# Cached attention for one token: head loops on every engine, wo's first rows in seven loads, the result stored as four rows

## The chip, the cores and the metric

The kernel runs on one core of one Trainium2 chip. The metric is the device time of one execution in microseconds (us); the median of several runs is compared. The profile comes from one more execution, taken by the hardware profiler. The engines are PE (TensorE), DVE (VectorE), ACT (ScalarE), POOL (GpSimd) and SP (SyncE, which here only issues DMAs). ACT issues a few DMAs too. The core has 16 DMA engines.

## What is computed

One decode step for one token x of 576 numbers. Its layernorm xn goes through two branches, and both are added to x. All data are float32.

```python
q = (xn @ wq).reshape(32 heads, 128)                       # wq: 576 x 4096
scores = einsum("hd,hkd->hk", q, k_cache) * 128 ** -0.5     # k_cache: 32 x 16384 x 128
o = einsum("hk,hkd->hd", softmax(scores), v_cache)          # v_cache: 32 x 16384 x 128
attention = o.reshape(4096) @ wo                            # wo: 4096 x 576
geglu = (gelu(xn @ w_gate) * (xn @ w_up)) @ w_down          # 576 x 4608, 576 x 4608, 4608 x 576
out = x + attention + geglu
```

K and V are 8.39 MB for each head, 537 MB for 32 heads; the weights make up the rest of the 587.6 MB that the kernel reads. Each number is used once.

## The kernel before, in words

Three SBUF slots of 64 KB per partition (`slot_a`, `slot_b`, `slot_v`, lines 124 to 126) take everything that is loaded. A load fills 128 partitions; partition p of a head holds its positions 128p to 128p + 127, 64 KB in one piece.

**Order.** There is no scheduler: the class `Order` (line 39) works out for each instruction which semaphores it must wait for, and hangs the last wait on the instruction itself; earlier ones become instructions of their own (line 91 and line 106). SP issues its DMAs in program order, so a DMA that waits holds up all that stand behind it.

**Projections (lines 224 to 327).** The weights wq, w_gate and w_up come into the slots; PE multiplies them with xn spread over 32 columns. q stays in PSUM (`qb`). `ffn` writes gate and up, and `ffn_act` (line 319) makes `hT` = gelu(gate) * up on DVE and ACT.

**Heads (lines 342 to 394).** K of the even heads comes into `slot_b`, of the odd ones into `slot_a`, V into `slot_v`. SP's order is K(0) as two halves of 64 columns, K(1), V(0), K(2), V(1) and so on: K(h+2) waits until DVE has read K(h), V(h) until PE has read V(h-1). For each head:

- DVE multiplies the slot by q, broadcast from `qs` (two halves, one for even and one for odd heads), and sums over 128 columns into `scores` (line 368 and 369, recorded at line 214); then `reduce_max` (line 384) and, after a transpose on PE, the maximum of one row (line 386).
- ACT copies the sums of the head before from PSUM (`z`), copies the next q to `qs`, scales the maximum (`nb`), takes exp into `pe` with its sum in `lsum`, copies the output column of the head before to `oall` and fetches the q after next (`qcur`).
- PE runs a hardware loop of 32 turns already (line 342): q broadcast (line 334, `pqs`), transpose (line 346), the maximum broadcast, the diagonal sums of the head before (`out_steps`, line 329), and 32 products of `pe` with V (`po`, line 334).

DVE, ACT and SP have all 32 heads written out one after the other. `hold` (line 137) puts the start of DVE's code on a multiple of 128 instructions and arms a hint for the branch in `release` (line 143), a loop of two turns at the end; line 160 aligns SP's code in the same way.

**Tail (lines 396 to 468).** w_down's first 28 rows per partition go to `slot_b`, where DVE sums them weighted with `hT`; V(31) follows, then the last 8 rows of w_down and wo, in pieces of 8, 12, 4, 4, 2, 1 and 1 rows per partition (`WO_PIECES`, line 32). One row is 576 numbers, 2304 bytes. PE multiplies each row with its column of `hT` or `oT` (`add_out`, line 435). DVE copies the sums (four rows of 144 numbers, on partitions 0, 32, 64 and 96) to `o4`, and SP and ACT store two rows each, with one DMA. SP then waits for both (line 134).

Of the kernel before, what the change touches and what calls it, by code (L numbers as in the profile page):

```python
# [10 lines left out]
ALU = mybir.AluOpType  # L11
# [19 lines left out]
WD_A = 28  # L31
WO_PIECES = (8, 12, 4, 4, 2, 1, 1)
WO_A = 20
# [84 lines left out]
@with_exitstack  # L118
def kernel(ctx: ExitStack, tc: tile.TileContext, x, k_cache, v_cache, wq, wo, wg, wu, wd, out):
    nc = tc.nc  # L120
    ends = tc.alloc_semaphore("ends")
    slots = []
    for i, name in enumerate(("slot_a", "slot_b", "slot_v")):
        t = nc.alloc_sbuf_tensor_at(name, [P, R * DH], F32, offset=SLOT_AT + i * SLOT_B)
        SIZES[t.name] = R * DH
        slots.append(t.ap())
    i = nc.sync.dma_start(slots[0], wq[:DM].rearrange("(p j) f -> p (j f)", j=DJ)).then_inc(ends, 32)
# [6 lines left out]
    nc.sync.wait_ge(ends, 32)  # L134


def hold(engine):

    engine.addr_align(128, offset=0, max_nops=0)
    return engine.mark_branch_hint_location()  # L140


def release(nc, kind, engine, place):
    only = OrderedEngineSet([kind])
    name = f"release_{nc.next_id()}"
    turns = nc.alloc_registers(f"{name}_i", engines=only)
    nc.regs_mov(turns, 0)
    nc.br(f"{name}_loop", engines=only)
    with nc.body(f"{name}_loop", valid_engines=only):
        engine.nop()  # L150
        nc.regs_alu(turns, turns, 1, op=ALU.add)
        engine.br_lt(turns, 2, on_true=f"{name}_loop", on_false=f"{name}_end").branch_hint(place)
    nc.switch_bb(f"{name}_end")


def decode(tc, x, k_cache, v_cache, wq, wo, wg, wu, wd, out, slots, s_ends):
    nc = tc.nc
    o = Order(tc)
    place = hold(nc.vector)
    nc.sync.addr_align(128, offset=0, max_nops=0)  # L160
    names = iter(range(1000))
# [31 lines left out]
    z = sbuf("z", P, 512)  # L193
    qcur, qs = sbuf("qcur", 1, DH), sbuf("qs", P, 2 * DH)
    S = sbuf("scores", P, 2 * R)
    lsum, oall = sbuf("lsum", P, H), sbuf("oall", P, H)
    gu, hT = sbuf("gu", P, 2 * WD_T), sbuf("hT", P, WD_T)
# [27 lines left out]
    ROW3 = 3 * DF  # L225
    nc.tensor.wait_ge(s_ends, 32).then_inc(s_ends, -32)
    qt = load(sb[:, ROW3 : ROW3 + QS], wtail["q"])
# [15 lines left out]
    o.op("vector", lambda e: e.memset(eps_t, EPS), eps_t)  # L243
    for bank in (PO, pc, pq):
        o.op("vector", lambda e, bank=bank: e.memset(bank, 0.0), bank)
    dve("tensor_reduce", par, ident.rearrange("p (d s) -> p s d", s=2), axis=AX.X, op=ALU.add)
# [45 lines left out]

    def q_of(h):
        return qs[:, h % 2 * DH : h % 2 * DH + DH]

    s_q, s_m, s_n, s_o, s_e, s_v = (tc.alloc_semaphore(f"to_pe_{n}") for n in "qmnoev")
    act(qcur, q_part(0))
    pe_op(pq[:, :DH], ones[:1, :], qcur, True, True)
    act(q_of(0), pq[:, :DH])
    act(qcur, q_part(1), signal=s_q)  # L300

# [30 lines left out]
    def chain(steps):  # L332
        for k, (dst, lhs, rhs, start, stop) in enumerate(steps):
            i = nc.tensor.matmul(dst, lhs, rhs, start=start, stop=stop)  # L334
        return i.then_inc(o.sem["tensor"], 1)

    def take(s, n=1):
        nc.tensor.wait_ge(s, n).then_inc(s, -n)  # L338

    o.wait("tensor", [ident, ones, same], [pg, pc, PO, pq])  # L340
    base, marks = o.count["tensor"], 5
    with nc.Fori(0, H, engines=OrderedEngineSet([mybir.EngineType.PE]), head_slot={mybir.EngineType.PE: 0}):
        take(s_q)
        chain([(pq[:, :DH], ones[:1, :], qcur, True, True)])
        take(s_m)
        nc.tensor.transpose(pt[:1, :P], pm, ident).then_inc(o.sem["tensor"], 1)  # L346
        take(s_n)
        chain([(pb[:, :1], ones[:1, :], nm[:1], True, True)])
        take(s_o)
        chain(out_steps(0))  # L350
        take(s_e)
        take(s_v, 16)
        chain([(PO[32 * (k % 4) : 32 * (k % 4) + 4, :], pe[:, 4 * k : 4 * k + 4], sv[:, 512 * k : 512 * k + 512], k < 4, k >= 28)
               for k in range(32)])
    o.count["tensor"] = base + marks * H

    def ran(h, mark, out, *ins):
        o.note("tensor", o.sem["tensor"], base + marks * h + mark, ins, [out])

    s_k = [sem() for _ in range(2)]  # L360
    times = [0, 0]
    for h in range(H):
        s = h % 2
        kt, n = (sb, sa)[s], R if h else SUB
        for i in range(0, R, n):
            if h:
                times[s] += 16
            part = kt[:, i * DH : (i + n) * DH]
            o.dma(part, kv[h][:, i * DH : (i + n) * DH], s_k[s] if h else sem(), times[s] or 16)
        if h:  # L370
            o.dma(sv, vv[h - 1], s_v, 0)
            ran(h - 1, 5, PO, pe, sv)
        sc = S[:, s * R : s * R + R]
        for i in range(0, R, n):
            blk = kt[:, i * DH : (i + n) * DH].rearrange("p (n d) -> p n d", d=DH)
            dve("tensor_mul", blk, blk, q_of(h).unsqueeze(1).to_broadcast([P, n, DH]))
            dve("tensor_reduce", sc[:, i : i + n], blk, axis=AX.X, op=ALU.add)
        if h == 0:
            ffn_act()
        act(z, PO, signal=s_o)  # L380
        ran(h, 1, pq[:, :DH], ones, qcur)
        if h + 1 < H:
            act(q_of(h + 1), pq[:, :DH])
        o.op("vector", lambda e: e.reduce_max(pm, sc, axis=AX.X), pm, sc, signal=s_m)
        ran(h, 2, pt[:1, :P], pm, ident)
        o.op("vector", lambda e: e.tensor_reduce(nm[:1], pt[:1, :P], axis=AX.X, op=ALU.max, negate=True), nm[:1], pt[:1, :P], signal=s_n)  # L386
        ran(h, 3, pb[:, :1], nm[:1])
        act(nb, pb[:, :1], scale=SCALE)
        act(pe, sc, AF.Exp, signal=s_e, bias=nb, scale=SCALE, accum_out=lsum[:, h : h + 1])
        ran(h, 4, pc[:, :1], z, same)  # L390
        if h:
            act(oall[:, h - 1 : h], pc[:, :1])
        if h + 1 < H:
            act(qcur, q_part(min(h + 2, H - 1)), signal=s_q)
# [10 lines left out]
    o.dma(sv, vv[H - 1], s_v, 0)  # L405
    ran(H - 1, 5, PO, pe, sv)
    wd_rows = load_rows(sa, 0, wdv, WD_A, WD_T - WD_A)
    wo_rows, lo = [], 0
    for n in WO_PIECES:
        wo_rows += load_rows(sa, WD_T - WD_A + lo, wov, lo, n) if lo < WO_A else load_rows(sb, 1 + lo - WO_A, wov, lo, n)  # L410
        lo += n

    act(z, PO)
    for s in out_steps(H - 1):
        pe_op(*s)
    act(oall[:, H - 1 :], pc[:, :1])

# [3 lines left out]
    dve("reciprocal", rl, pl)  # L421
    dve("tensor_mul", on, oall, rl)
    dve("tensor_mul", onx.rearrange("p (h r) -> p h r", r=4), on.unsqueeze(2).to_broadcast([P, H, 4]),
# [68 lines left out]
```

## Time and profile before

| what | us |
|---|---|
| median of 3 runs (1364.1 to 1364.12) | 1364.12 |
| the profiled execution | 1364.24 |
| its span, first to last instruction | 1362.5 |
| outside the span | 1.74 |
| DVE busy | 1158.3 |
| PE busy | 444.2 |
| ACT busy | 63.2 |

The read rate over the span is 431 GB/s. In the rows of the profile, `L214` is line 214 of the kernel; since helpers record the operations, many rows share a line, and the names of the tiles (out<-in) tell them apart. PEld is the loading of weights into PE, SPq and ACTq are the DMA queues of SP and ACT, PEq is PE's sequencer. Idle time of an engine stands with what ended it. The DMA share is the mean busy share of the 16 DMA engines; in short stretches it can be over 1, since a packet is counted where it starts or ends.

### The profile page before, as it was taken

What the parts mean: (1) busy time and instruction counts of PE and PEld (TensorE: products, weight loads), DVE (VectorE), ACT (ScalarE), POOL (GpSimd) and SP (SyncE); (2) the same over time, 40 slices, a digit from 0 to 9 for tenths busy, and PEclk for the clock granted to TensorE, in tenths of its full rate; (3) what the DMA queues carried; (4) which work ended last, traced back from release to release, by engine and by line L of the source; (5) the groups of instructions that cost most, each with busy time, mean ns of one, the idle gap of its engine ahead of it and who ended that gap; (6) DMA issues with size and microseconds to landing.
All of it is one profiled execution on the core that took longest, in us unless ns stands there. A gap on an engine that the chain in (4) does not pass through costs nothing.

```text
span 1362.5 us, 6978 instructions
## 1 busy us (share of the span) xinstructions
PE 444.2 (33%) x3012; PEld 161.2 (12%) x3012; DVE 1158.3 (85%) x195; ACT 63.2 (5%) x231; POOL 1.0 (0%) x7
## 2 busy tenths in 40 slices
PE   2431233332322333323222333333223333232236
PEld 1110111110101111101111111001111111011112
DVE  1069999899888888899888888998888888988882
ACT  0000000000000000000000000000000000000000
POOL 0000000000000000000000000000000000000000
PEclk9675666666556666665556666665566666665569
DMA  9999999999999999999999999999999999999998
GB/s 402 445 426 435 444 435 433 433 431 433 433 433 433 439 439 435 435 431 433 433 431 433 433 444 435 433 433 433 433 433 433 433 439 439 435 433 431 434 432 347
DMA packets 11831, 587.72 MB, mean 431 GB/s; under 512 B 1319, under 2 KB 1325, under 8 KB 1710
## 3 DMA queue, kind: packets, MB, share of 16 engines
q1 hardware_dynamic: 11812, 587.60, 99.6%
q8 instruction: 5, 0.08, 0.0%
q14 instruction: 4, 0.03, 0.0%
q10 hardware_dynamic: 10, 0.01, 0.0%
HBM read 587.60 MB, written 0.00 MB: 431 GB/s over the span
## 4 chain that ended last, share of the span: by engine, by line
DMA 49%; DVE 39%; issue 0%; PE 0%; DVEq 0%
DMA slot_b<-in_A_k_cache_dram 43%; DVE slot_b L214 20%; DVE scores L214 19%; DMA slot_b<-in_B_w_down_dram 3%; DMA slot_b<-in_A_wo_dram 3%; PE pg L211 0%; PE pg L346 0%; DVE z L214 0%; DVEq L91 0%; DVE nm L386 0%
## 5 line engine op out<-in xcount | busy, mean ns | idle before, releaser
L334 PE MATMUL po<-slot_v,pe 128*4 128x512 f32 x2048 | 292.9, 736 | 607.4 <-PEq L338 607.4
L214 DVE TENSOR_TENSOR slot_a<-slot_a,qs 128x16384 f32<-128x16384 f32 x16 | 275.6, 17223 | 42.6 <-DMA slot_a<-in_A_k_cache_dram 42.6
L214 DVE TENSOR_TENSOR slot_b<-slot_b,qs 128x16384 f32<-128x16384 f32 (+1 forms) x17 | 275.7, 16218 | 39.2 <-DMA slot_b<-in_A_k_cache_dram 39.2
L214 DVE TENSOR_REDUCE scores<-slot_b 128x128 f32<-128x16384 f32 (+1 forms) x17 | 275.7, 16216 | 0.6
L214 DVE TENSOR_REDUCE scores<-slot_a 128x128 f32<-128x16384 f32 x16 | 275.5, 17220 | 0.6
L334 PEld LDWEIGHTS po<-slot_v,pe 128*4 128x4 f32 x2048 | 56.5, 99 | 816.8 <-issue 816.8
L346 PE MATMUL pg<-ident,pm 128*1 128x128 f32 x32 | 11.9, 371 | 240.0 <-PEq L338 240.0
L219 ACT ACTIVATE z<-po 128x512 f32<-128x512 f32 x33 | 19.7, 597 | 889.1 <-PE po L334 889.1
L334 PE MATMUL pc<-same,z 128*128 128x1 f32 x256 | 59.8, 355 | 0.0
L334 PEld LDWEIGHTS pc<-same,z 128*128 128x128 f32 x256 | 57.1, 328 | 0.5
L214 DVE TENSOR_TENSOR slot_v<-pg,same 128x396 f32<-128x396 f32 (+1 forms) x6 | 3.4, 558 | 51.7 <-PE pg L211 51.5
L346 PEld LDWEIGHTS pg<-ident,pm 128*1 128x1 f32 x32 | 2.5, 79 | 245.2 <-issue 245.2
L386 DVE TENSOR_REDUCE nm<-pg 1x1 f32<-1x128 f32 x32 | 8.9, 279 | 17.8 <-PE pg L346 17.8
L214 DVE SCALAR_TENSOR_TENSOR slot_b<-slot_b,hT 128x576 f32<-128x576 f32 x27 | 22.1, 819 | 0.9
L334 PE MATMUL pg<-nm,ones 1*128 1x1 f32 x64 | 17.6, 342 | 14.8 <-PEq L338 14.8
L334 PEld LDWEIGHTS pg<-nm,ones 1*128 1x128 f32 x64 | 15.8, 306 | 24.2 <-issue 24.2
L219 ACT ACTIVATE nb<-pg 128x1 f32<-128x1 f32 x32 | 5.5, 171 | 237.1 <-PE pg L334 237.1
L334 PE MATMUL pqs<-qcur,ones 1*128 1x128 f32 x64 | 15.4, 321 | 1.3 <-PEq L338 1.3
L211 PE MATMUL pg<-slot_b,z 128*32 128x396 f32 (+1 forms) x72 | 8.8, 660 | 17.5 <-DMA slot_b<-in_B_w_gate_dram 17.5
L219 ACT ACTIVATE pe<-scores,nb 128x128 f32<-128x128 f32 x32 | 12.9, 402 | 1.0
L334 PEld LDWEIGHTS pqs<-qcur,ones 1*128 1x128 f32 x64 | 9.4, 182 | 28.7 <-issue 28.7
L214 DVE COPY small<-pc 128x5 f32<-128x5 f32 x1 | 0.2, 164 | 13.1 <-PE pc L211 13.1
(75 smaller groups left out, 119.9 us busy)
## 6 DMA issues: line engine op xcount, KB each, us to landing
slot_b<-in_A_k_cache_dram SPq DMA_DIRECT2D x2, 4096.0 KB, 22.8
slot_b<-in_B_w_down_dram SPq DMA_DIRECT2D x1, 8064.0 KB, 42.4
slot_b<-in_B_w_gate_dram SPq DMA_DIRECT2D x1, 6912.0 KB, 54.9
slot_a<-in_B_w_up_dram SPq DMA_DIRECT2D x1, 6912.0 KB, 38.1
slot_a<-in_A_wo_dram SPq DMA_DIRECT2D x1, 3456.0 KB, 41.3
slot_v<-in_B_w_gate_dram SPq DMA_DIRECT2D x1, 2304.0 KB, 28.6
slot_v<-in_B_w_up_dram SPq DMA_DIRECT2D x1, 2304.0 KB, 36.9
slot_a<-in_B_w_down_dram SPq DMA_DIRECT2D x1, 2304.0 KB, 28.5
```

Of the source, the lines that this page charges most:

```text
L211: o.op("tensor", lambda e: e.matmul(outp, lhsT, rhs, start=start, stop=stop), outp, lhsT, rhs, signal=signal)
L214: o.op("vector", lambda e: getattr(e, name)(out, *ins, **kw), out, *[a for a in ins if isinstance(a, bass.AP)], *[a for a in kw.values() i ...
L219: o.op("scalar", lambda e: e.activation(out, src, func, **kw), out, src, kw.get("bias") if isinstance(kw.get("bias"), bass.AP) else None, ...
L334: i = nc.tensor.matmul(dst, lhs, rhs, start=start, stop=stop)
L346: nc.tensor.transpose(pt[:1, :P], pm, ident).then_inc(o.sem["tensor"], 1)
L386: o.op("vector", lambda e: e.tensor_reduce(nm[:1], pt[:1, :P], axis=AX.X, op=ALU.max, negate=True), nm[:1], pt[:1, :P], signal=s_n)
```

## The change

The change writes the heads as hardware loops on SP (two heads a turn, 15 turns), DVE (two heads a turn, 16 turns) and ACT (five loops, cut where q's row in PSUM changes), beside the one that PE has. Inside a loop the waits are explicit: `take` waits for a semaphore and takes its count down again, as an instruction of its own. Addresses that depend on the turn come from registers. With that:

- K(0) is one load, and `ffn_act` stands ahead of the heads.
- `qs` has one half; ACT writes it after DVE's multiplication of the head before (`s_qf`).
- PE ends each head with a drain that tells SP that V is read (`s_vf`); `po` itself tells ACT (`s_po`).
- `oall` has a column more, since the first turn writes an empty one.
- The aligned starts of DVE and SP are gone; DVE and ACT have the hint and the `release` loop, which now stands after the stores.
- wo's first 8 rows per partition are two pieces of 4. The first of these comes by seven loads: partitions 0 to 29 in five loads of six, partitions 30 and 31 in one, partitions 32 to 127 in one.
- Each of the four rows of the result is stored by a DMA of its own, two from SP and two from ACT; the semaphore at the end counts to 64.

The core of the diff:

```diff
-WO_PIECES = (8, 12, 4, 4, 2, 1, 1)
+WO_PIECES = (4, 4, 12, 4, 4, 2, 1, 1)
+WO_LOW = (0, 6, 12, 18, 24, 30, 32, P)
...
-    place = hold(nc.vector)
-    nc.sync.addr_align(128, offset=0, max_nops=0)
+    places = [e.mark_branch_hint_location() for e in (nc.vector, nc.scalar)]
...
-    kv = k_cache.rearrange("b h (p n) d -> (b h) p (n d)", p=P)
-    vv = v_cache.rearrange("b h (p n) d -> (b h) p (n d)", p=P)
+    kv, vv = (c.rearrange("b h (p n) d -> p (b h) (n d)", p=P) for c in (k_cache, v_cache))
...
+    def take(e, s, n=1):
+        e.wait_ge(s, n).then_inc(s, -n)
...
+    ffn_act()
...
+    def load_k(h, dst, s):
+        nc.sync.dma_start(dst, kv[:, head(h), :].rearrange("p h f -> p (h f)")).then_inc(s_k[s], 16)
+
+    def load_v(h):
+        nc.sync.dma_start(sv, vv[:, head(h), :].rearrange("p h f -> p (h f)")).then_inc(s_v, 16)
+
+    for h, dst in ((0, sb), (1, sa)):
+        o.wait("sync", [], [dst])
+        load_k(h, dst, h)
+    o.wait("sync", [], [sv])
+    load_v(0)
+    with nc.sync.Fori(0, (H - 2) // 2) as i:
+        for s, dst in ((0, sb), (1, sa)):
+            take(nc.sync, s_kf)
+            load_k(i * 2 + (2 + s), dst, s)
+            take(nc.sync, s_vf)
+            load_v(i * 2 + (1 + s))
+
+    with nc.Fori(0, H, engines=OrderedEngineSet([KIND["tensor"]]), head_slot={KIND["tensor"]: 0}):
...
         chain([(PO[32 * (k % 4) : 32 * (k % 4) + 4, :], pe[:, 4 * k : 4 * k + 4], sv[:, 512 * k : 512 * k + 512], k < 4, k >= 28)
-               for k in range(32)])
+               for k in range(32)], s_po)
+        nc.tensor.drain().then_inc(s_vf, 1)
+
+    with nc.vector.Fori(0, H // 2):
+        for s, kt in ((0, sb), (1, sa)):
+            blk = kt.rearrange("p (n d) -> p n d", d=DH)
+            sc = S[:, s * R : s * R + R]
+            take(nc.vector, s_k[s], 16)
+            take(nc.vector, s_qd)
+            nc.vector.tensor_mul(blk, blk, qs.unsqueeze(1).to_broadcast([P, R, DH])).then_inc(s_d, 1)
+            nc.vector.wait_ge(s_d, 1).then_inc(s_qf, 1)
+            nc.vector.tensor_reduce(sc, blk, axis=AX.X, op=ALU.add).then_inc(s_d, 1)
+            nc.vector.wait_ge(s_d, 2).then_inc(s_kf, 1)
+            take(nc.vector, s_d, 2)
+            nc.vector.reduce_max(pm, sc, axis=AX.X).then_inc(s_m, 1)
+            take(nc.vector, s_pt)
+            nc.vector.tensor_reduce(nm[:1], pt[:1, :P], axis=AX.X, op=ALU.max, negate=True).then_inc(s_n, 1)
+
+    for h0, n in ((0, 6), (6, 8), (14, 8), (22, 8), (30, 2)):
+        row, lo = divmod(min(h0 + 2, H - 1), H // 4)
+        with nc.scalar.Fori(0, n) as i:
+            take(nc.scalar, s_po)
+            nc.scalar.activation(z, PO, AF.Copy).then_inc(s_o, 1)
+            take(nc.scalar, s_pq)
+            take(nc.scalar, s_qf)
+            nc.scalar.activation(qs, pq[:, :DH], AF.Copy).then_inc(s_qd, 1)
+            take(nc.scalar, s_pb)
+            nc.scalar.activation(nb, pb[:, :1], AF.Copy, scale=SCALE).then_inc(s_a, 1)
+            take(nc.scalar, s_a)
+            nc.scalar.activation(pe, S[:, bass.ds(i % 2 * R, R)], AF.Exp, bias=nb, scale=SCALE, accum_out=lsum[:, bass.ds(i + h0, 1)]).then_inc(s_e, 1)
+            take(nc.scalar, s_pc)
+            nc.scalar.activation(oall[:, bass.ds(i + h0, 1)], pc[:, :1], AF.Copy)
...
-    def load_rows(t, at, src, lo, n):
-        load(t[:, at * D : (at + n) * D], src[:, lo * D : (lo + n) * D])
+    def load_rows(t, at, src, lo, n, cuts=(0, P)):
+        for a, b in zip(cuts, cuts[1:]):
+            load(t[a:b, at * D : (at + n) * D], src[a:b, lo * D : (lo + n) * D])
...
+    take(nc.sync, s_kf)
     first = load_rows(sb, 0, wdv, 0, WD_A)
...
-    release(nc, mybir.EngineType.DVE, nc.vector, place)
-    for g in range(2):
-        o.dma(of[:, 2 * g * QUART : 2 * (g + 1) * QUART].rearrange("o (a f) -> (o a) f", a=2), o4[64 * g : 64 * g + 64 : 32, :], s_ends,
-              eng=("sync", "scalar")[g], out=True)
+    for g in range(4):
+        o.dma(of[:, g * QUART : (g + 1) * QUART], o4[32 * g : 32 * g + 1, :], s_ends, eng=("sync", "scalar")[g % 2], out=True)
+    release(nc, KIND["vector"], nc.vector, places[0])
+    release(nc, KIND["scalar"], nc.scalar, places[1])
```

More of the change, by code (lines that the diff above doesn't have):

```diff
@@ L126 @@
         slots.append(t.ap())
-    i = nc.sync.dma_start(slots[0], wq[:DM].rearrange("(p j) f -> p (j f)", j=DJ)).then_inc(ends, 32)
+    i = nc.sync.dma_start(slots[0], wq[:DM].rearrange("(p j) f -> p (j f)", j=DJ)).then_inc(ends, 64)
     tc.no_tile_sem_insts.add(i.ins.name)
@@ L133 @@
     tc.no_sync_barrier()
[L134 to L140, printed above, removed]
+    nc.sync.wait_ge(ends, 64)
+KIND = {"vector": mybir.EngineType.DVE, "scalar": mybir.EngineType.Activation, "tensor": mybir.EngineType.PE}
 def release(nc, kind, engine, place):
@@ L193, in decode @@
     z = sbuf("z", P, 512)
-    qcur, qs = sbuf("qcur", 1, DH), sbuf("qs", P, 2 * DH)
+    qcur, qs = sbuf("qcur", 1, DH), sbuf("qs", P, DH)
     S = sbuf("scores", P, 2 * R)
-    lsum, oall = sbuf("lsum", P, H), sbuf("oall", P, H)
+    lsum, oall = sbuf("lsum", P, H), sbuf("oall", P, H + 1)
     gu, hT = sbuf("gu", P, 2 * WD_T), sbuf("hT", P, WD_T)
@@ L243, in decode @@
     o.op("vector", lambda e: e.memset(eps_t, EPS), eps_t)
-    for bank in (PO, pc, pq):
-        o.op("vector", lambda e, bank=bank: e.memset(bank, 0.0), bank)
+    s_q, s_m, s_n, s_o, s_e, s_v, s_po, s_pq, s_pt, s_pb, s_pc, s_vf, s_kf, s_qf, s_qd, s_d, s_a = (
+        tc.alloc_semaphore(f"h{n}") for n in range(17))
+    s_k = [tc.alloc_semaphore(f"k{n}") for n in range(2)]
+    for bank, s in ((PO, s_po), (pc, None), (pq, None)):
+        o.op("vector", lambda e, bank=bank: e.memset(bank, 0.0), bank, signal=s)
     dve("tensor_reduce", par, ident.rearrange("p (d s) -> p s d", s=2), axis=AX.X, op=ALU.add)
@@ L291, in q_part @@
         return qb[r : r + 1, lo : lo + DH]
[L293 to L296 removed]
     act(qcur, q_part(0))
     pe_op(pq[:, :DH], ones[:1, :], qcur, True, True)
[L299 removed]
+    act(qs, pq[:, :DH], signal=s_qd)
     act(qcur, q_part(1), signal=s_q)
@@ L330, in out_steps, with chain @@
         return [(pc[:, :1], z[:, j * DH : (j + 1) * DH], same[:, j : j + 1], j == 0, j == 3) for j in range(4)]
-    def chain(steps):
-        for k, (dst, lhs, rhs, start, stop) in enumerate(steps):
+    def chain(steps, s):
+        for dst, lhs, rhs, start, stop in steps:
             i = nc.tensor.matmul(dst, lhs, rhs, start=start, stop=stop)
-        return i.then_inc(o.sem["tensor"], 1)
-    def take(s, n=1):
-        nc.tensor.wait_ge(s, n).then_inc(s, -n)
-    o.wait("tensor", [ident, ones, same], [pg, pc, PO, pq])
@@ L341, in decode @@
[L341 to L352, printed above, removed]
-        chain([(PO[32 * (k % 4) : 32 * (k % 4) + 4, :], pe[:, 4 * k : 4 * k + 4], sv[:, 512 * k : 512 * k + 512], k < 4, k >= 28)
-               for k in range(32)])
@@ L355, in decode @@
[L355 to L394, printed above, removed]
@@ L396, in load_rows, with head @@
-    def load_rows(t, at, src, lo, n):
-        load(t[:, at * D : (at + n) * D], src[:, lo * D : (lo + n) * D])
+        i.then_inc(s, 1)
+    def take(e, s, n=1):
+        e.wait_ge(s, n).then_inc(s, -n)
+    def head(h):
+        return bass.ds(h, 1)
+    ffn_act()
+    o.wait("tensor", [ident, ones, same], [pg, pc, PO, pq])
+    o.wait("vector", [qs], [S, pm, nm])
+    o.wait("scalar", [qb], [z, qs, nb, pe, lsum, oall, qcur])
+    def load_k(h, dst, s):
+        nc.sync.dma_start(dst, kv[:, head(h), :].rearrange("p h f -> p (h f)")).then_inc(s_k[s], 16)
@@ new lines, in decode @@
+    with nc.Fori(0, H, engines=OrderedEngineSet([KIND["tensor"]]), head_slot={KIND["tensor"]: 0}):
+        take(nc.tensor, s_q)
+        chain([(pq[:, :DH], ones[:1, :], qcur, True, True)], s_pq)
+        take(nc.tensor, s_m)
+        nc.tensor.transpose(pt[:1, :P], pm, ident).then_inc(s_pt, 1)
+        take(nc.tensor, s_n)
+        chain([(pb[:, :1], ones[:1, :], nm[:1], True, True)], s_pb)
+        take(nc.tensor, s_o)
+        chain(out_steps(0), s_pc)
+        take(nc.tensor, s_e)
+        take(nc.tensor, s_v, 16)
+        chain([(PO[32 * (k % 4) : 32 * (k % 4) + 4, :], pe[:, 4 * k : 4 * k + 4], sv[:, 512 * k : 512 * k + 512], k < 4, k >= 28)
+               for k in range(32)], s_po)
+        nc.tensor.drain().then_inc(s_vf, 1)
@@ new lines, in decode @@
+    for h0, n in ((0, 6), (6, 8), (14, 8), (22, 8), (30, 2)):
[12 more added lines that the diff above has]
+            nc.scalar.activation(oall[:, bass.ds(i + h0, 1)], pc[:, :1], AF.Copy)
+            src = q_part(min(h0 + 2, H - 1)) if n == 2 else qb[32 * row : 32 * row + 1, bass.ds(i * DH + lo * DH, DH)]
+            nc.scalar.activation(qcur, src, AF.Copy).then_inc(s_q, 1)
@@ L404, in decode @@
         dve("scalar_tensor_tensor", total, first[j], hT[:, j : j + 1], total, op0=ALU.mult, op1=ALU.add)
-    o.dma(sv, vv[H - 1], s_v, 0)
-    ran(H - 1, 5, PO, pe, sv)
+    take(nc.sync, s_vf)
+    load_v(H - 1)
+    take(nc.sync, s_kf)
     wd_rows = load_rows(sa, 0, wdv, WD_A, WD_T - WD_A)
```

10 lines of the change are left out of this document (6 added, 4 removed).

## The prediction, written before the result was known

> **What bounds the kernel now.** I read the page's busy table and its DMA rows first, then stretches of the run, then the chain of waits, then the start and the tail in order of time. The page:
>
> ```profile
> span 1362.5 us, 6978 instructions
> ...
> PE 444.2 (33%) x3012; PEld 161.2 (12%) x3012; DVE 1158.3 (85%) x195; ACT 63.2 (5%) x231; POOL 1.0 (0%) x7
> ...
> DMA  9999999999999999999999999999999999999998
> ```
>
> Busy time by stretch (columns: stretch, length, busy time of PE, PEld, DVE, ACT, POOL, clock, DMA share, GB/s):
>
> ```profile
> 2.60:70.00 67.40, 28.23 (x240) 10.77 (x244) 7.42 (x20) 3.55 (x6) 0.00 (x0) 0.85 0.99 425
> 70.00:140.00 70.00, 18.92 (x161) 6.99 (x157) 57.90 (x17) 1.71 (x7) 0.00 (x0) 0.61 1.00 431
> 140.00:1270.00 1130.00, 360.20 (x2260) 128.80 (x2252) 1032.77 (x119) 54.44 (x205) 0.00 (x0) 0.61 1.00 434
> 1270.00:1356.00 86.00, 34.12 (x304) 13.45 (x307) 59.66 (x38) 3.51 (x13) 0.00 (x0) 0.68 0.99 427
> ```
>
> From 1.7 us to 1356 us the 16 DMA engines have no free time: share 0.99 to 1.00, 434 GB/s in the loop, 27.1 for each engine. DVE is busy 85% but waits for data in every head; one head in order of time, with the wait in brackets:
>
> ```profile
> 1234.89 17.23 DVE L214 TENSOR_TENSOR slot_b<-slot_b,qs 128x16384 f32<-128x16384 f32 x1 [2.95 <-DMA slot_b<-in_A_k_cache_dram]
> ...
> 1252.15 17.22 DVE L214 TENSOR_REDUCE scores<-slot_b 128x128 f32<-128x16384 f32 x1
> ...
> 1254.24 9.74 PE L334 MATMUL po<-slot_v,pe 128*4 128x512 f32 x64 [19.81 <-PEq L338]
> ...
> 1263.91 0.48 PE L334 MATMUL pqs<-qcur,ones 1*128 1x128 f32 x2
> ...
> 1264.05 0.33 SPq L107 DMA_DIRECT2D slot_v<-in_A_v_cache_dram  x1
> ...
> 1264.55 0.27 ACT L219 ACTIVATE qs<-pqs 128x128 f32<-128x128 f32 x1
> ...
> 1269.40 0.33 SPq L107 DMA_DIRECT2D slot_b<-in_B_w_down_dram  x1
> ...
> 1273.57 17.23 DVE L214 TENSOR_TENSOR slot_a<-slot_a,qs 128x16384 f32<-128x16384 f32 x1 [3.04 <-DMA slot_a<-in_A_k_cache_dram]
> ```
>
> A head is 1273.57 - 1234.89 = 38.68 us, its K and V 2 x 8.39 MB / 434 GB/s = 38.66 us: the loop runs at the DMA's pace. So the time is the start of the stream, its bytes (unchanged), any hole in it, and the tail:
>
> ```profile
> 1356.00:1356.50 0.50, 0.50 (x24) 0.43 (x18) 0.00 (x0) 0.00 (x0) 0.00 (x0) 1.00 0.89 350
> 1356.50:1357.00 0.50, 0.50 (x20) 0.21 (x13) 0.00 (x0) 0.00 (x0) 0.00 (x0) 1.00 0.64 226
> 1357.00:1357.50 0.50, 0.50 (x20) 0.23 (x16) 0.00 (x0) 0.00 (x0) 0.00 (x0) 1.00 0.33 129
> 1357.50:1358.00 0.50, 0.50 (x23) 0.18 (x12) 0.00 (x0) 0.00 (x0) 0.00 (x0) 1.00 0.19 74
> 1358.00:1358.50 0.50, 0.29 (x8) 0.00 (x0) 0.00 (x0) 0.00 (x0) 0.00 (x0) 1.00 0.02 9
> ```
>
> The end in order of time:
>
> ```profile
> 1358.56 0.43 PE L211 MATMUL pg<-slot_b,oT 128*1 128x144 f32 x8 [0.28 <-DMA slot_b<-in_A_wo_dram]
> 1359.14 0.31 DVE L214 COPY z<-pg 128x144 f32<-128x144 f32 x1 [3.78 <-PE pg L211]
> 1359.47 0.60 SPq L107 DMA_DIRECT2D out_dram<-z  x1
> 1359.48 0.59 ACTq L107 DMA_DIRECT2D out_dram<-z  x1
> ```
>
> The 16 engines do not finish together: about six are through by 1356.75 (share 0.64), three still run at 1357.75 (0.19 x 16), one works past 1358.0. The last matmuls wait for that one. The shares after 1356.0 add up to 0.5 x (0.89+0.64+0.33+0.19+0.02) = 1.04 us, so perfectly level engines would be through at 1357.04, some 1.1 to 1.2 us earlier. Apart from that, only the store is left.
>
> **The change, part by part.** The profiled execution took 1364.24 us, 1.74 outside its span; the median of the runs is 1364.12, that is 0.12 less. I make the sum as a difference and set it on the median.
>
> Steady loop: 0. SP, DVE and ACT now wait by instructions of their own instead of waits attached to the work. The chain of waits shows one of these on DVE:
>
> ```profile
> 1234.80 0.03 issue
> 1234.82 0.02 DVEq L91
> 1234.85 0.04 issue
> ```
>
> 0.06 us each beyond the first; DVE has six a head, at most 0.36 us, against 2.95 to 3.04 us in which it waits for K. PE's own loop, 9.74 us of matmuls from 1254.24 and the next head's at 1263.91, shows nothing for a jump back. The V load, now behind a PE drain, is issued at 1264.05 in before and its data start when K lands at 1273.5: 9 us of cover. The next K load (here the w_down load at 1269.40) has V's 19.3 us ahead of it. `qs` is single now, but its copy (1264.55) came after the multiplication that read it ended (1252.12) and 9 us ahead of the next; exp falls into the 19.81 us in which PE waits for V. If any cover were gone, its overrun would stop all 16 engines once a head.
>
> Start: 0. Head 0's K is one load instead of two halves, so DVE starts after all of it. The first head loads on SP's queue, and V's time from issue to landing:
>
> ```profile
> 66.38 2.31 SPq L107 DMA_DIRECT2D slot_b<-in_A_k_cache_dram  x2
> ...
> 86.10 0.33 SPq L107 DMA_DIRECT2D slot_v<-in_A_v_cache_dram  x1
> 120.74 0.33 SPq L107 DMA_DIRECT2D slot_b<-in_A_k_cache_dram  x1
> ```
>
> ```profile
> slot_v<-in_A_v_cache_dram SPq DMA_DIRECT2D x1, 47.6
> ```
>
> The kernel's first load and DVE's first multiplication, and the stretch from that load's issue on:
>
> ```profile
> 0.74 0.46 SPq L127 DMA_DIRECT2D slot_a<-in_A_wq_dram  x1
> ...
> 86.00 8.67 DVE L214 TENSOR_TENSOR slot_b<-slot_b,qs 128x8192 f32<-128x8192 f32 x1
> ```
>
> ```profile
> 0.74:1.70 0.96, 0.00 (x0) 0.00 (x0) 0.00 (x0) 0.00 (x0) 0.15 (x1) 1.00 0.00 0
> ```
>
> V of head 0 lands at 86.10 + 47.6 = 133.7, so K of head 0 is whole at 133.7 - 2 x 19.33 = 95.0. DVE began at 86.00; now at 95.1. Two passes of 17.22 and their waits end at 129.7; SP issues K of head 2 at 129.9 instead of 120.74. The first load shows 1.0 us from issue (0.74) to data (none before 1.70): 130.9. The engine that ends first is free of V at about 131.6 (133.7 less the spread of 2.1 above), the last at 133.7. It fits by 0.7 us for the earliest engine and 2.8 for the latest, which sets the end; a small hole on early engines costs nothing, since they wait for the late one at the tail. Then DVE gains some 2.7 us a head (3.0 less 0.3), so the next issue has 3 us more room. The GELU steps move into the gap before 95.0. SP and DVE lose their aligned starts; everything then still waits for wq.
>
> Split of wo's rows 0 to 3: -0.25. A partition's piece is 9216 bytes, 0.34 us at 27.1 GB/s. In before each engine gets 8 of the 128 pieces. No row of before shows how many engines a transfer of six or two partitions uses. If it is spread like the others over 16, nothing moves: 0. If it stays on as many engines as it has partitions, always the same ones, two engines get 12 pieces (+1.36 us), four get 11 (+1.02) and ten get 6 (-0.68). Best case: the six are those through by 1356.75; they end by 1357.6 to 1358.1, the late ten by 1357.5: -0.35 to -0.1. Worst: the last engine is one of the six, +1.02 to +1.36. The trace does not name the engines. I take -0.25, nearer the best end, because ten of 16 are relieved and one alone works past 1358.0.
>
> [...]
>
> The seven transfers instead of one cost SP at most 6 x 0.60 us, and they are issued long before their data can flow:
>
> ```profile
> 1308.44 0.91 SPq L107 DMA_DIRECT2D slot_a<-in_A_wo_dram  x2
> ...
> 1315.76 7.63 SPq L107 DMA_DIRECT2D slot_b<-in_A_wo_dram  x5
> ...
> 1331.22 8.80 PE L334 MATMUL po<-slot_v,pe 128*4 128x512 f32 x64 [19.53 <-PEq L338]
> ```
>
> Issues reach 1313, before DVE frees slot_b at 1315.76 and before V ends at 1331. Hidden.
>
> Store: +0.16. Each queue issues two one-row DMAs instead of one two-row DMA.
>
> ```profile
> L107 ACTq DMA_DIRECT2D x<-in_A_x_dram x2: 222/241/260, 2.1 to 2.3; - x2
> ```
>
> ```profile
> 1.52 0.52 ACTq L107 DMA_DIRECT2D slot_v<-in_A_x_dram  x1
> ```
>
> One-row issues took 0.52 (first) and 0.24, so 0.76 against 0.60. Ends: two at 0.24 give -0.12, two at 0.60 give +0.60. The two release loops come after and run beside the landing.
>
> Sum: -0.25 + 0.16 = -0.09: 1364.12 - 0.09 = **1364.0 us**.
>
> **The rivals.**
>
> (1) The last engine is loaded, not relieved: 1.2 + 0.16 on the median, 1365.5. For it: six of 16 engines are loaded, so the last is among them six times in 16, and every engine that ends within 1 us of it decides just as well (three at 1357.75). Against: ten of 16 are relieved, and a single engine works past 1358.0.
>
> (2) The split does nothing, because it is spread evenly or a middle engine (through near 1357.25, then 1358.3 to 1358.6) takes over: 0 to +0.4, about 1364.3.
>
> (3) Slower for good: DVE becomes the bound in its loop. It decides from 3.0 us more a head. The mechanism is code fetched again at a jump back: a 16 KB fetch takes 0.6 us of an engine behind a 64 KB piece of 2.4 us, so 3 us; twice in each turn of two heads adds 3 us a head with 0.36 for waits: (3.36 - 3.0) x 31 = 11 us, 1375. At 4 us a head it is 1395. Against it, the DMA rows of 100 to 1300 us, in which PE's loop turned some 30 times:
>
> ```profile
> q14 instruction: 2, 0.02, 0.0%
> ```
>
> Two instruction packets of 8 KB are no fetch a turn. [...]
>
> **How the numbers follow.** Forecast 0.48, with its own range 1363.6 to 1364.7 (the store's two ends and -0.35 to 0 for the split). Rival 1: 0.25. Rival 2: 0.17. Rival 3: 0.08. A gain beyond 2.7 us: 0.02; level engines and the cheapest store give 1.2 + 0.12 only. The range reaches from 1363.3 to 1366.0: below, half of the levelling beyond my best case; above, rival 1 with the dearest store. 0.2% is 2.7 us, about what a measurement of this kernel can tell from no change: faster 0.02, same 0.90, slower 0.08.
>
> **What would show it.** DMA share 1.00 from 140 to 1270 us, DVE idle of 2.5 to 3.0 us a head and no instruction packets there: the loops are free. Share under 0.99 in 130 to 135 us: the start failed. The windows after 1355 us: right if the last engine is through before 1358.2; wrong if one works past 1359. First store issue to end of span: 3.03 us in before, 3.2 by my sum. A head longer than 38.7 us makes the prediction wrong.

## The result, and the profile after

The changed kernel takes 1371.84 us (median of 4 runs, 1370.77 to 1372.88) against 1364.11 us (4 runs, 1364.1 to 1364.12): ratio 1.0057, 95% interval 1.0044 to 1.0069. It is 7.73 us slower; the forecast was 1364.0 and the range ended at 1366.0. The profiled execution took 1371.21 us, its span is 1369.4 us.

The page of the changed kernel: span and instructions, busy time by engine, the DMA queues, and the two groups of DVE's multiplications with their idle time.

```profile
span 1369.4 us, 7788 instructions
...
PE 448.0 (33%) x3012; PEld 161.6 (12%) x3012; DVE 1158.4 (85%) x193; ACT 67.9 (5%) x234; POOL 1.0 (0%) x7
...
q1 hardware_dynamic: 11844, 587.60, 99.5%
q8 instruction: 5, 0.08, 0.0%
q10 hardware_dynamic: 10, 0.01, 0.0%
q14 instruction: 1, 0.01, 0.0%
...
L383 DVE TENSOR_TENSOR slot_b<-slot_b,qs 128x16384 f32<-128x16384 f32 x16 | 275.6, 17226 | 38.4 <-DVEq L334 38.4
L383 DVE TENSOR_TENSOR slot_a<-slot_a,qs 128x16384 f32<-128x16384 f32 x16 | 275.6, 17226 | 30.3 <-DVEq L334 30.3
```

Nothing here looks like a slower kernel: DVE's work is the same to 0.1 us, it still waits 68.7 us in 32 heads, and six instruction packets in all (88 KB) are no fetch per turn of a loop. So the loss is in the stream, and a table by stretch finds it (columns: stretch, length, busy time of PE, PEld, DVE, ACT, POOL, clock, DMA share, GB/s). Before:

```profile
128.00:138.00 10.00, 4.20 (x28) 0.90 (x32) 10.00 (x1) 0.00 (x0) 0.00 (x0) 0.56 0.98 426
...
1335.00:1345.00 10.00, 8.28 (x88) 3.21 (x84) 1.22 (x4) 0.97 (x3) 0.00 (x0) 1.00 1.02 441
```

After:

```profile
128.00:138.00 10.00, 6.98 (x35) 3.17 (x39) 9.07 (x4) 1.06 (x5) 0.00 (x0) 0.50 0.99 406
138.00:1270.00 1132.00, 363.32 (x2283) 129.36 (x2275) 1041.74 (x118) 58.07 (x205) 0.00 (x0) 0.61 1.00 434
1335.00:1345.00 10.00, 8.19 (x72) 2.83 (x68) 2.76 (x6) 0.77 (x2) 0.00 (x0) 0.94 1.00 237
```

Two places differ. In 1335 to 1345 us, where the seven loads of wo's first rows flow, the DMA share is still 1.00 but the rate is 237 GB/s instead of 441: the engines always have a piece in hand, and many pieces take longer. The packets of the trace show it one by one: a piece of 9216 bytes takes 0.35 us in the kernel before, and up to 1.11 us here, where 191 of 512 take over 0.4 us. The share counts the time of pieces, not bytes; whoever reads it alone misses this. (441 - 237) GB/s x 10 us = 2.0 MB, which is 4.7 us at 434 GB/s. The other place is at 128 to 138 us: 406 against 426. That reading is coarse, since three pieces of 64 KB make the difference. From 138 to 1270 us the rate is the same 434.

The second loss is easier to see as a lag. In order of time, the changed kernel at the start and in a late head (rows of DVE, SP and PE):

```profile
95.16 17.23 DVE L383 TENSOR_TENSOR slot_b<-slot_b,qs 128x16384 f32<-128x16384 f32 x1 [7.14 <-DVEq L334]
...
130.10 0.35 SPq L345 DMA_DIRECT2D slot_b<-in_A_k_cache_dram  x1
...
1236.59 17.23 DVE L383 TENSOR_TENSOR slot_b<-slot_b,qs 128x16384 f32<-128x16384 f32 x1 [2.59 <-DVEq L334]
...
1255.78 5.28 PE L330 MATMUL po<-slot_v,pe 128*4 128x512 f32 x21 [19.28 <-PEq L334]
```

Before, the same multiplication began at 1234.89 and the same V matmuls, which wait for the last engine, at 1254.24: the stream is 1.54 us late there. The semaphore events show where that arose: the last engine's part of V lands 0.96 us later than before for head 1, 1.11 and 1.26 us later for heads 2 and 3, and 1.5 us later from head 4 on.

The end, in order of time:

```profile
1365.31 0.43 PE L208 MATMUL pg<-slot_b,oT 128*1 128x144 f32 x8 [0.28 <-DMA slot_b<-in_A_wo_dram]
1365.88 0.31 DVE L211 COPY z<-pg 128x144 f32<-128x144 f32 x1 [2.19 <-PE pg L208]
1366.21 0.57 SPq L108 DMA_DIRECT2D out_dram<-z  x2
1366.22 0.55 ACTq L108 DMA_DIRECT2D out_dram<-z  x2
```

The last matmul starts 6.75 us later than before (1358.56); from the first store's issue to the end of the span are 3.19 us instead of 3.03.

### The profile page after: what moved, and what is told of

Its sections match the earlier page's. It is cut to its first block, busy times and chain, and to the rows that moved or that the text cites. A ratio compares the mean times of both kernels' runs of the same rounds, so it can differ in the third digit from the quotient of the medians.

```text
span 1369.4 us, 7788 instructions
## 1 busy us (share of the span) xinstructions
PE 448.0 (33%) x3012; PEld 161.6 (12%) x3012; DVE 1158.4 (85%) x193; ACT 67.9 (5%) x234; POOL 1.0 (0%) x7
## 5 line engine op out<-in xcount | busy, mean ns | idle before, releaser
L383 DVE TENSOR_TENSOR slot_b<-slot_b,qs 128x16384 f32<-128x16384 f32 x16 | 275.6, 17226 | 38.4 <-DVEq L334 38.4
L385 DVE TENSOR_REDUCE scores<-slot_b 128x128 f32<-128x16384 f32 x16 | 275.5, 17221 | 2.3
L388 DVE TENSOR_REDUCE pm<-scores 128x1 f32<-128x128 f32 x32 | 9.1, 286 | 8.2 <-DVEq L334 8.2
```

What stands on the lines that cost most here:

```text
L383: nc.vector.tensor_mul(blk, blk, qs.unsqueeze(1).to_broadcast([P, R, DH])).then_inc(s_d, 1)
L385: nc.vector.tensor_reduce(sc, blk, axis=AX.X, op=ALU.add).then_inc(s_d, 1)
L388: nc.vector.reduce_max(pm, sc, axis=AX.X).then_inc(s_m, 1)
```

## Experiments

**1. The changed kernel without the split.**

```
-WO_LOW = (0, 6, 12, 18, 24, 30, 32, P)
+WO_LOW = (0, P)
```

> The changed kernel with wo's first four rows of all partitions in one load (the pieces 4, 4, 12, ... stay), everything else as changed. Theory A, the split load slows all engines while it flows (225 to 249 GB/s in 1335 to 1345 us, mean landing of the last load 4.5 us later than the start hole explains): 4 to 5.5 us below the changed kernel, 1366.3 to 1367.9, and over 420 GB/s in 1335 to 1345 us. Rival B, only the uneven count of pieces per engine counts: at most 1.4 us below it, 1370.4 or more. Rival C, the loops and their small stalls make the loss: within 0.5 us of the changed kernel, 1371 to 1372.

Measured: 1366.0 us (1365.13 to 1367.14; ratio to before 1.0014, 1.0004 to 1.0024), 5.84 us below the changed kernel.

```profile
1335.00:1345.00 10.00, 8.19 (x67) 2.51 (x59) 3.13 (x6) 0.77 (x2) 0.00 (x0) 0.92 1.03 440
```

The rate is back at 440 GB/s. Theory A holds, with 0.3 us more than its range allowed; rivals B and C are too small to be the loss. 1.9 us above before remain.

**2. The kernel before with only the split.**

```
-WO_PIECES = (8, 12, 4, 4, 2, 1, 1)
+WO_PIECES = (4, 4, 12, 4, 4, 2, 1, 1)
+WO_LOW = (0, 6, 12, 18, 24, 30, 32, P)
```

(with the changed `load_rows`)

> The kernel before with only the split of wo's first four rows per partition (seven loads for them, then the other four rows by one load). Theory A: 4 to 5.5 us above before, 1368.1 to 1369.6, with under 300 GB/s while the seven loads flow. Rival B, uneven counts alone: between -0.35 and +1.4 us, 1363.8 to 1365.5. Rival C, the loops make the loss: within 0.3 us of before, 1364.1.

Measured: 1370.16 us (1.0043, 1.0028 to 1.0057): +6.06 us alone, somewhat more than I gave.

```profile
1335.00:1345.00 10.00, 8.27 (x64) 2.89 (x60) 1.23 (x4) 0.95 (x3) 0.00 (x0) 0.84 1.04 257
```

So the split needs nothing of the rest of the change to cost what it costs.

**3. The same rows in four loads of 32 neighbours**, `WO_LOW = (0, 32, 64, 96, P)` in the kernel before.

> The kernel before with the same four rows in four loads of 32 partitions each. If such a load spreads over 16 engines, two partitions each, every engine has 8 pieces as in one load: rival B (uneven counts) expects no change, within 0.3 us of 1364.1. Theory A1, several engines that write into the same neighbouring partitions at once slow each other: 32 partitions are a quarter of the destination, so the loads flow at half the rate, some 2.7 us more (4 x 0.68 us of data at 434 GB/s taking twice that), 1366 to 1368. Theory A2, the slowness comes from loads of fewer than 16 partitions alone: within 0.5 us of before.

Measured: 1369.55 us (1.004, 1.0026 to 1.0055), +5.45.

```profile
1335.00:1345.00 10.00, 8.27 (x92) 3.25 (x88) 0.84 (x3) 0.96 (x3) 0.00 (x0) 1.00 1.00 241
```

A2 falls: 32 partitions are enough to be slow. A1 has the sign right and the size too small by half. The landing of each of these loads shows 16 semaphore events, which fits two partitions for each engine: counts are even here, and B falls again. In experiment 2, as in the changed kernel, each load of six shows six such events while its data land, and the load of two shows two, which fits six and two engines and uneven counts. The load of 96 shows 16 in the changed kernel, which fits six partitions for each engine. That all loads of six use the same engines, as the counts 12, 11 and 6 have it, is an estimate: the trace does not name the engine of a piece.

**4. K of head 0 as a whole, no loops.**

```
-SUB = 64
+SUB = R
```

> The kernel before with K of head 0 waited for as a whole (one load, one multiplication, one reduction) and no loops. Theory: the K load of head 2 is issued near 129.5 us instead of 120.7 and finds engines already empty; the stream loses what the changed kernel lost at that place, 0.9 to 1.5 us: 1365.0 to 1365.6, DMA share under 0.8 in 132 to 134 us. Rival: the hole comes from the DMA in SP's loop with its address in a register: no hole here, 1364.1 within 0.3.

Measured: 1365.3 us (1.0009, 0.9999 to 1.0019), +1.2; the interval just touches no change, but the fastest run here (1364.52) is slower than the slowest of before (1364.37).

```profile
129.50 0.33 SPq L107 DMA_DIRECT2D slot_b<-in_A_k_cache_dram  x1
...
1255.27 5.11 PE L334 MATMUL po<-slot_v,pe 128*4 128x512 f32 x24 [19.88 <-PEq L338]
```

The load of K of head 2 goes out at 129.50, and 1.03 us of lag is there in the late head, without a loop and without an address in a register. The second loss comes with the whole K(0), as the theory had it; experiment 8 takes it away again.

**5. Eight loads of 16 neighbours**, `WO_LOW = [slice(16 * i, 16 * i + 16) for i in range(8)]` in the kernel before.

> The kernel before with the same four rows in eight loads of 16 neighbouring partitions. Every engine still has eight pieces of 9216 bytes if such a load uses 16 engines, one partition each. [...] Rival S (small loads are slow because there are more of them, with fewer pieces each): some cost that grows with the number of loads, 1366 to 1372, and the same for the next kernel. Rival B (uneven counts): nothing, 1364.1.

Measured: 1368.94 us (1.0036, 1.0023 to 1.0048), +4.8, no more than with loads of 32.

```profile
1335.00:1345.00 10.00, 8.28 (x88) 3.21 (x84) 0.94 (x4) 0.96 (x3) 0.00 (x0) 1.00 1.01 238
```

The estimate of rival S is wrong: its cost should have grown with the number of loads, and eight cost 4.8 us where four cost 5.45. An eighth of the partitions at a time flows at 238 GB/s, a quarter at 241. Several of these loads are in flight together, so 16 and 32 neighbours may well crowd the same places; that is a reading after the fact, and no run here tests it by itself. Theory P in the next experiments is A1 without its size: engines that write into neighbouring partitions at once slow each other.

**6. Eight loads, seven of them of every seventh partition.**

```
+WO_LOW = [slice(i, i + 106, 7) for i in range(7)] + [slice(112, P)]
```

> The kernel before with the same four rows in eight loads of 16 partitions each, but seven of them take every seventh partition (0, 7, ... 105, then 1, 8, ... 106, and so on), and only the last one takes 16 neighbours (112 to 127). The number of loads, the pieces per load and per engine are those of the kernel with eight loads of neighbours. Theory P: the 16 writers are spread over almost all of the destination, so most of the cost goes: 1364.5 to 1366.5. Rival S (number and size of the loads): the same time as with neighbours, within 1 us of it.

Measured: 1381.12 us (1.0126, 1.0109 to 1.0143), +17. SP's rows, and the stretch in which the loads flow:

```profile
1308.13 39.39 SPq L108 DMA_DIRECT2D slot_a<-in_A_wo_dram  x6
```

```profile
1337.00:1355.00 18.00, 10.21 (x80) 3.53 (x72) 0.84 (x3) 0.97 (x3) 0.00 (x0) 0.75 0.25 67
```

This answers nothing of the question: the kernel's record of tile use takes interleaved partitions for overlapping ones, so every load waited for the landing of the one ahead (DMA share 0.25, issues 2.5 us apart). Repeated below without those waits.

**7. Neighbours as destination, every seventh partition's rows as source**: the loads of experiment 5 with the source slices of experiment 6.

> Eight loads of 16 neighbouring partitions as destination, but each takes the rows of wo in HBM that the strided kernel takes (every seventh partition's), so that partitions get each other's rows and the product of these four rows is not the reference's. Theory P (the destination decides): the time of the kernel with neighbours on both sides, within 1 us of it. Rival H (the addresses in HBM decide: neighbours' rows lie 73,728 bytes apart, every seventh 516,096): the time of the strided kernel, within 1 us of it.

Measured: 1369.89 us (1.0043, 1.0026 to 1.006), 0.95 us from experiment 5.

```profile
1335.00:1345.00 10.00, 8.27 (x68) 2.94 (x64) 1.20 (x4) 0.97 (x3) 0.00 (x0) 0.84 1.00 228
```

Slow as with neighbours on both sides, whatever the HBM addresses. The comparison with the strided kernel had to wait for experiment 9.

**8. Loops without the split, head 0 outside DVE's loop.** From experiment 1's kernel:

```
+    s_k0 = tc.alloc_semaphore("k_first")
...
+            nc.sync.dma_start(dst[:, :half], kv[:, head(0), :half].rearrange("p h f -> p (h f)")).then_inc(s_k0, 16)
+            nc.sync.dma_start(dst[:, half:], kv[:, head(0), half:].rearrange("p h f -> p (h f)")).then_inc(s_k[0], 16)
...
+    dve_head(0, sb, SUB)
+    with nc.vector.Fori(0, H // 2 - 1):
+        dve_head(1, sa, R)
+        dve_head(0, sb, R)
+    dve_head(1, sa, R)
```

> The changed kernel with one load for wo's first four rows, and head 0 taken out of DVE's loop with its K in two halves as in before; all other loops and the four stores stay. Theory: K of head 2 is issued near 121 us again and the 1.2 us of the start go, so the kernel with one load (1366.0) falls to before plus the store: 1364.1 to 1364.6. Rival: the loops themselves lose time (the extra 0.3 us or more that the sum of the parts does not yet show): 1365 or more.

Measured: 1364.01 us (0.9999, 0.9989 to 1.0009), 1.99 below experiment 1 and level with before.

```profile
123.06 0.35 SPq L346 DMA_DIRECT2D slot_b<-in_A_k_cache_dram  x1
...
1254.05 6.30 PE L331 MATMUL po<-slot_v,pe 128*4 128x512 f32 x44 [19.25 <-PEq L335]
```

The load goes out at 123.06 and the lag is gone. All other loops and the four stores are still there and cost nothing; the rival falls.

**9. Experiment 6 without its waits**: all loads of the split back to back on one semaphore.

```
+        dst, s = t[:, at * D : (at + n) * D], sem()
+        o.wait("sync", [], [dst])
+        for c in cuts:
+            nc.sync.dma_start(dst[c], src[c, lo * D : (lo + n) * D]).then_inc(s, 16)
+        o.note("dma", s, 16 * len(cuts), [], [dst])
```

> Eight loads of 16 partitions, seven of them of every seventh partition, as before, but now issued back to back, all on one semaphore, so that none waits for the one ahead. Theory P (engines that write into neighbouring partitions at once slow each other; spread writers don't): most of the 4.8 us that eight loads of neighbours cost go, 1364.3 to 1366.5, and over 380 GB/s in 1335 to 1345 us. Rival S (any load of fewer partitions is slow, wherever it writes): 1368 to 1370, under 300 GB/s there.

Measured: 1367.87 us (1.0028, 1.0018 to 1.0039), +3.74.

```profile
1335.00:1345.00 10.00, 8.27 (x68) 3.04 (x64) 1.05 (x4) 0.96 (x3) 0.00 (x0) 0.84 1.02 299
```

Neither theory's number: faster than neighbours (299 GB/s against 238), but far from free.

**10. Four loads of every fourth partition**, `WO_LOW = [slice(i, P, 4) for i in range(4)]`, issued as in experiment 9.

> Four loads of 32 partitions each, as in the kernel with four loads of neighbours (1369.55), but each takes every fourth partition (0, 4, ... 124, then 1, 5, ... 125, and so on), back to back on one semaphore. Theory P: 1364.3 to 1367 (two partitions per engine, four apart, so some engines may still meet). Rival S: 1368.5 to 1370.

Measured: 1364.24 us (1.0002, 0.9992 to 1.0011), +0.1.

```profile
1335.00:1345.00 10.00, 8.28 (x68) 3.00 (x64) 0.97 (x4) 0.96 (x3) 0.00 (x0) 0.84 1.04 441
```

The full rate. Four loads, 32 partitions each, as in experiment 3, are 5.3 us faster when each takes every fourth partition. Rival S falls; neither the number of loads nor partitions per load is the cause. The way of issuing differs from experiment 3 too; experiment 16 closes that gap.

**11. Experiment 8 with two two-row stores**, and **12. before with four one-row stores** (only the store loops exchanged).

> The kernel with loops, head 0 outside DVE's loop with K in halves, one load for wo's first four rows, and the result stored by two two-row transfers as in before. If the loops cost nothing and four stores cost 0.16 us: 1363.7 to 1364.1, the lowest of all kernels here by at most 0.3 us. If the number of stores doesn't matter: 1364.0, as with four stores. If the loops lose time hidden by a gain elsewhere, nothing below 1364.1 comes of it.

> The kernel before with only the result stored by four one-row transfers, two on each queue. My sum: +0.16 us, 1364.25; from the first store's issue to the end of the span 3.2 us instead of 3.03. Ends of the range: -0.12 and +0.60. Rival: a second transfer's completion adds a whole issue-to-landing of its own, over +1 us, 1365.1 or more.

Measured: 1364.35 us (1.0002, 0.9993 to 1.0011) and 1363.9 us (0.9999, 0.999 to 1.0008). The stores of experiment 12, whose span ends at 1361.9:

```profile
1359.19 0.64 SPq L107 DMA_DIRECT2D out_dram<-z  x2
1359.20 0.52 ACTq L107 DMA_DIRECT2D out_dram<-z  x2
```

2.71 us from first issue to the end. Four stores stand 0.23 and 0.34 us below two, with no cost in either pair, though the intervals don't part them from no change. The same four kernels, paired the other way, put the loops at 0.1 to 0.2 us dearer, which the intervals don't part from nothing either; experiment 11 lies above the 1363.7 to 1364.1 that free loops were to give. No kernel here is measurably faster than before.

**13. Two loads of 64 neighbours**, `WO_LOW = [slice(0, 64), slice(64, P)]`, issued as in experiment 9, like the kernels of experiments 14 to 16.

> The kernel before with wo's first four rows in two loads of 64 neighbouring partitions each, four partitions per engine if such a load uses 16 engines in order. [...] Rival N (only engines within four neighbouring partitions meet; here each engine has four neighbours for itself): no cost, 1364.0 to 1364.5.

Measured: 1369.04 us (1.0032, 1.0022 to 1.0042), +4.86.

```profile
1335.00:1340.00 5.00, 5.00 (x48) 1.03 (x40) 0.10 (x1) 0.00 (x0) 0.00 (x0) 0.94 0.99 184
1340.00:1345.00 5.00, 3.27 (x28) 2.09 (x28) 0.84 (x3) 0.97 (x3) 0.00 (x0) 0.74 1.04 293
```

N falls: half of the partitions at a time are nearly as slow as a quarter, +4.86 us against +5.45 in experiment 3. The trace's packets account for the cost. Of the pieces of 9216 bytes, 192 take longer than 0.4 us, 0.72 us on average, where every one of the split's pieces in experiment 10 takes 0.35. At most 128 of the 192 are the split's own, so pieces of the next load, in flight beside them, are slow too, and some of 18432 bytes of the load ahead take up to 2.0 us instead of 0.69. The extra time of all pieces from 1325 us on, against the 0.35, 0.69 and 1.03 us that the three sizes take in the kernel before, is 4.9 us for each of the 16 engines.

**14. Loads of 32 and 96 neighbours**, `[slice(0, 32), slice(32, P)]`, and **15. the sixes apart**, `[slice(i, i + 26, 5) for i in range(5)] + [slice(30, 32), slice(32, P)]`.

> The kernel before with the four rows in two loads, of 32 and of 96 neighbouring partitions (the change has the same 96, but six loads for the 32). Every engine has two and six pieces, eight in all. If the load of 96 carries the cost of the split: 3 us or more above before, 1367 to 1370. If the loads of six and two carry it: under 1.5 us, 1364.1 to 1365.6. Uneven counts play no part here.

> The kernel before with the split of the change, but the five loads of six take partitions five apart (0, 5, ... 25, then 1, 6, ... 26, and so on); 30 and 31 and the load of 96 as changed, all on one semaphore. Pieces per engine are exactly those of the change (12, 11, 6). If the crowding of six engines on neighbouring partitions carries the cost of 6.06 us: at most 1.4 us above before (the uneven counts), 1364.1 to 1365.6. If the load of 96 carries it: 1367 to 1370.

Measured: 1368.15 us (1.0027, 1.0018 to 1.0037) and 1369.59 us (1.0037, 1.0026 to 1.0048). One row of each:

```profile
1335.00:1345.00 10.00, 8.27 (x84) 3.22 (x80) 1.12 (x4) 0.97 (x3) 0.00 (x0) 0.95 1.01 276
```

```profile
1335.00:1345.00 10.00, 8.27 (x66) 2.87 (x62) 1.04 (x4) 0.96 (x3) 0.00 (x0) 0.84 1.02 254
```

Without any load of six, +4.0 us of the 6.06 remain; with the sixes spread, +5.4. So the cost is mostly not the sixes' crowding. The pair 32 and 96 carries two thirds; six loads instead of one add 1.4 to 2 us. The landings of the last wo load show what that is. They run from 1356.52 to 1358.52 us in the kernel before, from 1360.48 to 1362.45 in experiment 14, from 1360.45 to 1363.91 in experiment 2 and from 1360.30 to 1363.48 in experiment 15. The first engine ends alike in the last three; the last engine ends 1.0 to 1.5 us later where the counts are uneven.

**16. Four loads of 32 neighbours from every fourth partition's rows.**

> Four loads of 32 neighbouring partitions as destination, their rows taken from every fourth partition's place in wo, so the product of these four rows is not the reference's. If the destination decides: the time of four loads of 32 neighbours, 1368.5 to 1370. If the addresses in HBM decide: the time of every fourth partition on both sides, 1364.0 to 1364.6.

Measured: 1369.12 us (1.0028, 1.0012 to 1.0044), the time of experiment 3.

```profile
1335.00:1345.00 10.00, 8.27 (x72) 3.10 (x68) 1.01 (x4) 0.97 (x3) 0.00 (x0) 0.84 1.00 248
```

With experiment 10's source addresses and way of issuing, and experiment 3's destination: slow. Only the destination's partitions differ from experiment 10, and 4.9 us with them. The partitions in SBUF decide, not the rows' places in HBM.

## Why the prediction was wrong, step by step

The 7.73 us are: split 1371.84 - 1366.0 = 5.84; start 1366.0 - 1364.01 = 1.99; the rest (loops and stores) 1364.01 - 1364.11 = -0.10.

- **Split, forecast -0.25, measured +5.84 (+6.06 alone).** The step that failed is "A partition's piece is 9216 bytes, 0.34 us at 27.1 GB/s". The slow pieces took 0.64 us on average in experiment 2 and 0.72 in experiment 13. I let the number of pieces per engine vary and held the time of one fixed; every bound, -0.35 to +1.36, counted pieces only. The runs show that the time of a piece depends on which partitions the loads in flight write: 441 GB/s with 128 partitions or every fourth, 228 to 276 with neighbours by 16, 32, 64 or 32 and 96, equal counts or not. Halves of the partitions (experiment 13) are slow, and loads of every fourth partition (experiment 10) are free. By an estimate from the rates, 237 and 441 GB/s, data at about half the rate cost their own time once more: for the split's 1.18 MB, 1.18 MB / 434 GB/s = 2.7 us; measured were 4.8 to 5.5. The rest is, as far as the packets tell, in the pieces of the loads ahead and behind, which are slowed as well (experiment 13). Why neighbours are slow, why the loads beside them suffer, and why every seventh partition still costs 3.74 us though its loads are spread too, was not shown.
- **Its rivals.** As times, the last engine loaded (1365.5) and no effect (1364.3) are both wrong: all engines were slowed. The first of the 16 landings of the last load came at 1361.48 us in the changed kernel instead of 1356.52, and the last at 1365.26 instead of 1358.52; the lag of the start is 1.54 us of that. As a mechanism, the first rival was there beside the failed step: each load of six shows six semaphore events, and the last engine ended 1.5 us later in experiment 2 than with one load of 32 in their place, where the forecast's -0.25 has it relieved. No run shows the ten relieved engines from which the -0.25 was worked out.
- **Seven issues on SP, hidden: right.** SP's rows of the changed kernel:

```profile
1310.30 3.27 SPq L108 DMA_DIRECT2D slot_a<-in_A_wo_dram  x9
1317.37 18.20 SPq L108 DMA_DIRECT2D slot_b<-in_A_wo_dram  x5
```

The issues end by 1336 instead of 1323, long ahead of their data; experiment 10, which pays nothing, has the same (15.80 us for the five).

- **Start, forecast 0, measured +1.99.** Up to the issue it was right: DVE from 95.16 (forecast 95.1), K of head 2 issued at 130.10 (129.9). The step that failed is "The first load shows 1.0 us from issue (0.74) to data (none before 1.70): 130.9", and with it "It fits by 0.7 us for the earliest engine". That 1.0 us is when the first engine begins. The same first load of the kernel before, a little further on (a piece counts in the stretch in which it starts):

```profile
1.70:2.00 0.30, 0.00 (x0) 0.00 (x0) 0.00 (x0) 0.00 (x0) 0.30 (x2) 1.00 7.38 2403
2.00:2.50 0.50, 0.00 (x0) 0.00 (x0) 0.17 (x2) 0.00 (x0) 0.33 (x2) 1.00 1.55 524
2.50:3.00 0.50, 0.00 (x0) 0.00 (x0) 0.44 (x1) 0.37 (x1) 0.00 (x0) 1.00 0.33 131
```

One engine begins only after 2.50, 1.8 us or more after the issue. In the changed kernel the first 16 pieces of K of head 2 begin between 1.2 and 3.6 us after it, by the trace's packets, and take 2.42 to 3.15 us where every such piece took 2.42 before. From 129 to 138 us an engine is idle for 0.36 us on average and loses 0.49 us by longer pieces; why the pieces are longer is not shown. The cost by issue time: none at 120.74 (before) and 123.06 (experiment 8), 1.2 us at 129.50 (experiment 4), 1.99 us at 130.14 (experiment 1). So the edge lies between 123 and 129.5, and not at the 130.6 that the forecast's 0.7 us of room would allow. Also wrong is "a small hole on early engines costs nothing": the last engine's V was late too, by 1.54 us for the rest of the run.
- **Steady loop, 0: right.** 434 GB/s from 138 to 1270 us, DVE waits 2.59 us in the late head (forecast 2.5 to 3.0), a head is unchanged; experiment 8 with all loops but head 0's is at 1364.01. Rival 3 (code fetched at jumps) is refuted by the six instruction packets: none of them lies between 100 and 1345 us, where the loops of the heads turn, so no fetch at a jump of theirs is seen. Its price was too low as well: the 16 KB packets of the kernel before took 0.88 to 1.12 us each, not 0.6.
- **Store, +0.16: not to be told from nothing.** The profiled execution shows 3.19 against 3.03 us as forecast, but experiments 11 and 12 put four stores 0.2 to 0.3 us below two; the sum's term has at best the right size.
- **What was to show it.** The sign of the tail worked: an engine was at work past 1359 us, with the last landing at 1365.26. "Share under 0.99 in 130 to 135 us" was no sign of a failed start: the share there is 0.94 in the changed kernel, but 0.97 in the kernel before, and 1.03 in experiment 1, which has the same start as the changed kernel. The rate in the same stretch tells the kernels with the loss from those without, though not its size: 419 GB/s before and in experiment 8, and 406, 393 and 367 in experiments 1 and 4 and the changed kernel.

## What to carry to other kernels

Beside a saturated stream, a load should not be cut into blocks of neighbouring partitions. That cost 4.0 to 6.06 us here alone: 228 to 276 GB/s instead of 441 while the loads flow, and in experiment 13 pieces of the load ahead took up to 2.0 us instead of 0.69. A cut along the free axis (two pieces of four rows for all partitions, experiment 8) or by every fourth partition (experiment 10) cost nothing here. Spreading alone is no rule, since every seventh partition cost 3.74 us. A saturated stream is judged by GB/s, since the DMA share stayed at 1.00 here while the rate fell to 237 GB/s. When a load is issued later, ask when its data start on the last engine, not on the first, and leave some microseconds.

## What was not expected of the hardware

Blocks of 16, 32 and 64 neighbours cost nearly the same (4.8, 5.45, 4.86 us), and the five later wo issues of SP took 18.20 us instead of 7.63 without any cost. The kernels with blocks of neighbours also vary more from run to run (experiment 13: 1367.95 to 1370.01) than the one with every fourth partition (1364.09 to 1364.42).
